# An attention and gated-MLP decode kernel: projection columns dealt p*8+j so that the output leaves without a transpose, and one row of the last weight matrix loaded early in 16 small DMAs

## The chip, the cores and the metric

The kernel runs on one core of a Trainium2 chip. The metric is the device time of one execution in microseconds (us), lower is better. Most executions of one kernel agree within 0.3%. Experiments sent together ran on one chip and share their runs of the kernel before; differences are taken within such a group only.

## The reference

One token is decoded. Block A is attention with 32 query heads on 4 K/V heads over a cache of 65,536 positions. Block B is a small gated MLP. A gate mixes them.

```python
g = sigmoid((x * gate_w).sum(-1))                  # x: [1, 1, 1024]
q = (x @ wq)                                       # wq: [1024, 4096], 32 heads of 128
p = softmax(q @ k_cache.T / sqrt(128))             # caches: [4 heads, 65536, 128] bf16, 64 MB each
a = (p @ v_cache).reshape(4096) @ wo               # wo: [4096, 1024]
b = mlp(x, w_in, w_sp, b_sp) @ w_out               # w_out: [1792, 1024]
out = g * a + (1 - g) * b                          # [1, 1, 1024] bf16
```

About 162 MB are read for 2 KB of output, so the kernel is in the main a stream of loads.

## The kernel before

Every large load goes through one helper on the SP queue, in tiles of 4 MB: 128 partitions with 32 KB each, one packet of 32 KB a partition. Five buffers rotate.

```python
def load(src, shape, name):
    t = kv.tile([P, CT * P], BF16, name=name, tag="kv")        # 5 buffers of 32 KB a partition
    ...
    nc.sync.dma_start(out=v, in_=src)
```

The loads are w_in, wq, then K and V by turns, then w_out, then wo. At the end the output projection runs. It uses blocks of the weight matrix as the stationary operand (each a weight load of 128 x 128 followed by one matmul with 64 copies of a column of the vector), so that the 1024 outputs come to lie in PSUM as 8 columns of 128 partitions:

```python
def project(w, n, vec, c0, first=False, last=False):
    for c in range(n):
        for j in range(NJ):                                     # NJ = 8
            nc.tensor.matmul(
                out_ps[:, j, :], lhsT=w[:, c, j * P:(j + 1) * P],   # 128 neighbouring columns
                rhs=vec[:, c0 + c:c0 + c + 1].to_broadcast([P, W]), ...)

project(load(B_w_out..., "wout_t"), FC, uT, 0, first=True)      # 14 rows per partition
wo_view = A_wo.rearrange("(p c) n -> p c n", c=OC)              # 32 rows of 2 KB per partition
c0 = 0
for split in WO_SPLIT:                                          # ((16,), (8, 4, 2, 1, 1))
    t = kv.tile(...)
    for n in split:
        nc.sync.dma_start(out=t[:, c0 - b:c0 - b + n, :], in_=wo_view[:, c0:c0 + n, :])
        project(t[:, c0 - b:c0 - b + n, :], n, oa, c0, last=(c0 + n == OC))
        c0 += n
out_sb = const.tile([P, NJ], FP32, name="out_sb")
nc.vector.tensor_copy(out=out_sb[:], in_=out_ps[:, :, 0])
outT_ps = psm.tile([NJ, P], FP32, name="outT_ps", tag="m")
nc.tensor.transpose(outT_ps[:], out_sb[:], ident_f[:])
outT = const.tile([NJ, P], BF16, name="outT")
nc.vector.tensor_copy(out=outT[:], in_=outT_ps[:])
nc.sync.dma_start(out=out.rearrange("o t (j p) -> (o t j) p", p=P), in_=outT[:])
```

Column j of `out_ps` holds outputs j*128 to j*128+127, one a partition. The transpose turns that into 8 rows of 256 bytes each.

One more part matters, because it is the only place of this kernel where weight columns are not neighbours: the first MLP matrix, whose stationary blocks take every 14th column (28 bytes apart).

```python
w = win_t[i][:, c, :].rearrange("p (h m f) -> p h f m", h=2, f=FC)       # FC = 14
nc.tensor.matmul(z_ps[...], lhsT=w[:, hf, f, :], rhs=..., ...)
```

Of the kernel before, what the change touches and what calls it, by code (L numbers as in the profile page):

```python
# [7 lines left out]
FP32 = mybir.dt.float32  # L8
BF16 = mybir.dt.bfloat16
# [5 lines left out]
P = 128  # L15
CT = 128
NKV = 5
TG = 8
CPS = 64
LAG = 4  # L20
EVAC_PAT = "vav"
WO_SPLIT = ((16,), (8, 4, 2, 1, 1))
SW = 256
W = 64
WL = 96
# [3 lines left out]
def kernel(  # L29
# [15 lines left out]
    nc = tc.nc  # L45

    _, _, D = A_x.shape
    _, G, S, DH = A_k_cache.shape
# [7 lines left out]
    OC = HD // P  # L56
    NJ = D // P
# [2 lines left out]
    NT = NCG // CT  # L60
    SCALE = float(DH) ** -0.5
    assert DH == P and D % P == 0 and FH % P == 0 and P % H == 0
    assert S % (P * CT) == 0 and CT % CPS == 0 and CPS % TG == 0 and sum(map(sum, WO_SPLIT)) == OC

    const = ctx.enter_context(tc.tile_pool(name="const", bufs=1))
    wk = ctx.enter_context(tc.tile_pool(name="wk", bufs=2))
# [5 lines left out]
    psm = ctx.enter_context(tc.tile_pool(name="psm", bufs=1, space=bass.MemoryType.PSUM))  # L72
# [3 lines left out]
    def load(src, shape, name):  # L76
        t = kv.tile([P, CT * P], BF16, name=name, tag="kv")
        n = 1
        for s in shape:
            n *= s  # L80
        v = t[:, :n]
        if len(shape) == 2:
            v = v.rearrange("p (a b) -> p a b", b=shape[1])
        nc.sync.dma_start(out=v, in_=src)  # L84
        return v

    def load_kv(src, g, j, name):
        k0 = j * CT * P
        return load(src[0, g, k0:k0 + CT * P, :].rearrange("(p c) d -> p c d", c=CT),
                    (CT, DH), name)  # L90

# [37 lines left out]
    def one_hot(shape, dtype, in0, col, name):  # L129
        t = const.tile(shape, dtype, name=name)  # L130
        nc.vector.tensor_scalar(out=t[:], in0=in0, scalar1=pf[:shape[0], col:col + 1],
                                scalar2=None, op0=ALU.is_equal)
        return t
# [4 lines left out]
    ident_f = one_hot([P, P], FP32, row[:], 0, "ident_f")  # L138
# [10 lines left out]
    for t in range(2):  # L149
        nc.vector.tensor_tensor(  # L150
            out=xm[:, t], in0=xb_ps[:, t * P:(t + 1) * P].rearrange("p (i c) -> p c i", c=KC),
# [82 lines left out]
    for c in range(KC):  # L234
        w = wq_t[c // KH]
# [142 lines left out]
    for g in range(G):  # L378
        for j in range(NT):
            ku = k_units(g, j, load_kv(A_k_cache, g, j, "kn"))  # L380
            for _ in ku:
                next(vu, None)
                run_step()
            rest(vu)
            if g > 0:
                vu = v_units(g - 1, j, load_kv(A_v_cache, g - 1, j, "vt"))
# [6 lines left out]
    for j in range(NT):  # L393
        rest(v_units(G - 1, j, load_kv(A_v_cache, G - 1, j, "vt")))


    out_ps = pss.tile([P, NJ, W], FP32, name="out_ps", tag="spt")

    def project(w, n, vec, c0, first=False, last=False):
        for c in range(n):  # L400
            for j in range(NJ):
                nc.tensor.matmul(  # L402
                    out_ps[:, j, :], lhsT=w[:, c, j * P:(j + 1) * P],
                    rhs=vec[:, c0 + c:c0 + c + 1].to_broadcast([P, W]),
                    start=(first and c == 0 and j == 0), stop=(last and c == n - 1),
                    skip_group_check=True)
# [9 lines left out]
    oa = const.tile([P, OC], BF16, name="oa")  # L416
    nc.vector.tensor_scalar(out=oa[:], in0=om_ps[:, :OC], scalar1=rl[:, 0:1], scalar2=gate,
                            op0=ALU.mult, op1=ALU.mult)

    project(load(B_w_out.rearrange("(p c) n -> p c n", c=FC), (FC, D), "wout_t"),  # L420
            FC, uT, 0, first=True)
    wo_view = A_wo.rearrange("(p c) n -> p c n", c=OC)
    c0 = 0
    for split in WO_SPLIT:
        t = kv.tile([P, CT * P], BF16, name="wo_t", tag="kv")
        t = t[:].rearrange("p (c n) -> p c n", n=D)
        b = c0
        for n in split:
            nc.sync.dma_start(out=t[:, c0 - b:c0 - b + n, :], in_=wo_view[:, c0:c0 + n, :])
            project(t[:, c0 - b:c0 - b + n, :], n, oa, c0, last=(c0 + n == OC))  # L430
            c0 += n
    out_sb = const.tile([P, NJ], FP32, name="out_sb")
    nc.vector.tensor_copy(out=out_sb[:], in_=out_ps[:, :, 0])  # L433
    outT_ps = psm.tile([NJ, P], FP32, name="outT_ps", tag="m")
    nc.tensor.transpose(outT_ps[:], out_sb[:], ident_f[:])
    outT = const.tile([NJ, P], BF16, name="outT")
    nc.vector.tensor_copy(out=outT[:], in_=outT_ps[:])
    nc.sync.dma_start(out=out.rearrange("o t (j p) -> (o t j) p", p=P), in_=outT[:])


    last = {}
# [37 lines left out]
```

## Time and profile before

| | before |
|---|---|
| time, median of the runs | 392.84 us |
| profiled span | 390.8 us |
| first 16 rows of wo complete | 377.70 us |
| last arrivals of wo, by DMA engine | 8 at 377.1 to 379.8, 8 at 385.9 to 387.4 us |
| copy of the result out of PSUM starts | 387.93 us |
| output DMA issued, its last arrival | 388.77, 389.96 us |

From the page of the kernel before: the span, the mean busy tenths of the 16 DMA engines in 40 slices, the GB/s in the same slices, and the groups of wo's matmuls and weight loads (busy us, mean ns of one, then idle time before them and its releaser).

```profile
span 390.8 us, 14957 instructions
...
DMA  8999999999999999999999999999999999999972
GB/s 329 426 444 429 441 426 430 434 429 428 429 428 426 431 423 431 429 434 429 424 426 436 424 429 431 423 434 423 428 427 434 436 434 429 434 421 428 433 330 114
...
L402 PE MATMUL out_ps<-oa,wo_t 128*128 128x64 bf16 x256 | 9.7, 204 | 6.1 <-DMA wo_t<-in_A_wo_dram 5.7
L402 PEld LDWEIGHTS <-wo_t 128*128 128x128 bf16 x256 | 9.4, 105 | 6.4 <-DMA wo_t<-in_A_wo_dram 5.8
```

The DMA engines are full from the second slice to the 38th: the load stream sets the time. Only the last two slices are not full. From the groups by line of the same kernel, the weight loads with strided columns (win_t) and with neighbouring ones (wq_t):

```profile
...
L185 PEld LDWEIGHTS <-win_t 128*128 128x128 bf16 x224 | 13.7, 158 | 1.3 <-DMA win_t<-in_B_w_in_dram 0.9 <-issue 0.4
...
L237 PEld LDWEIGHTS <-wq_t 128*128 128x128 bf16 x256 | 7.0, 104 | 7.6 <-DMA wq_t<-in_A_wq_dram 7.6
```

The strided ones have a mean of 158 ns, the others 104 ns. 224 strided pairs keep the engine busy 13.7 us, 61 ns each; 256 contiguous ones 7.0 us, 27 ns each.

The end of the kernel before in the timeline (start us, duration, engine, line, operation):

```profile
...
368.42 3.64 PE L402 MATMUL out_ps<-uT,wout_t 128*128 128x64 bf16 x112
...
377.75 7.13 PE L402 MATMUL out_ps<-oa,wo_t 128*128 128x64 bf16 x182 [5.69 <-DMA wo_t<-in_A_wo_dram]
385.29 2.61 PE L402 MATMUL out_ps<-oa,wo_t 128*128 128x64 bf16 x74 [0.41 <-issue]
...
387.93 0.17 DVE L433 COPY out_sb<-out_ps 128x8 f32<-128x8 f32 x1 [18.79 <-PE out_ps L402]
...
388.15 0.27 PE L435 MATMUL outT_ps<-ident_f,out_sb 128*8 128x128 f32 x1 [0.26 <-DVE out_sb L433]
388.46 0.28 DVE L437 CAST outT<-outT_ps 8x128 bf16<-8x128 f32 x1 [0.37 <-PE outT_ps L435]
388.77 0.36 SPq L438 DMA_DIRECT2D out_dram<-outT  x1
```

PE starts on wo at 377.75, 0.05 us after the first 16 rows are complete, and is done at 387.91, about half a microsecond after the last load (387.43). Copy, transpose, second copy and output DMA follow.

The last stretches of the kernel before. Columns: stretch, its length, busy time and count of PE, weight load, DVE, ACT and POOL, granted TensorE clock, DMA share, GB/s.

```profile
...
370.00:375.00 5.00, 2.06 (x67) 1.94 (x63) 0.00 (x0) 0.00 (x0) 0.00 (x0) 0.90 1.00 424
375.00:380.00 5.00, 2.25 (x43) 2.25 (x44) 0.00 (x0) 0.00 (x0) 0.00 (x0) 0.50 0.70 290
380.00:385.00 5.00, 4.88 (x144) 4.79 (x142) 0.00 (x0) 0.00 (x0) 0.00 (x0) 0.91 0.50 204
385.00:391.00 6.00, 2.88 (x75) 2.46 (x74) 0.45 (x2) 0.00 (x0) 0.00 (x0) 1.00 0.15 57
```

DMA share falls to 0.70 and then 0.50 long before the loads end: half of the engines have finished. The arrival records of wo's last row (one a DMA engine) say the same, eight by 379.8 us and eight more from 385.9 us on. The late ones are, as far as the packets can be told apart, those on which the 55 instruction-fetch packets of 16 KB (about 0.95 us each) fell.

### The profile page before, as it was taken

To read this page: it belongs to the slowest core of one execution; us is meant where nothing else is said; L and a number is where in the kernel's file an instruction comes from. 1 tells how busy PE (TensorE), PEld (TensorE's weight loads), DVE (VectorE), ACT (ScalarE), POOL (GpSimd) and SP (SyncE) were. 2 spreads that over 40 slices of the span, in tenths; PEclk is the share of its full clock that TensorE was granted. 3 is DMA by queue.
4 is the path that set the end of the run, shared out by engine and by line. 5 is a ranking of instruction groups with operands and counts; after the bars stand their busy time and mean duration, and the time that the engine had idled before them with its cause. 6 is when DMAs were issued, how large, how long until landed. Compare 5 with 4: busy or idle time off the path is not lost.

```text
span 390.8 us, 14957 instructions
## 1 busy us (share of the span) xinstructions
PE 306.5 (78%) x7080; PEld 296.8 (76%) x7080; DVE 152.3 (39%) x296; ACT 122.3 (31%) x139; POOL 1.0 (0%) x9
## 2 busy tenths in 40 slices
PE   0774379998888879778888888697979697996946
PEld 0764379887888779778888878696979697896846
DVE  2011036665684335336534543275434345300100
ACT  1010025554574323324543333244524242300000
POOL 1000000000000000000000000000000000000000
PEclk9999999999999989999999999899989899899869
DMA  8999999999999999999999999999999999999972
GB/s 329 426 444 429 441 426 430 434 429 428 429 428 426 431 423 431 429 434 429 424 426 436 424 429 431 423 434 423 428 427 434 436 434 429 434 421 428 433 330 114
DMA packets 6305, 162.96 MB, mean 417 GB/s; under 512 B 740, under 2 KB 740, under 8 KB 1124
## 3 DMA queue, kind: packets, MB, share of 16 engines
q1 hardware_dynamic: 6208, 162.01, 96.8%
q8 instruction: 55, 0.90, 0.8%
q14 instruction: 6, 0.05, 0.0%
q10 hardware_dynamic: 36, 0.00, 0.0%
HBM read 162.01 MB, written 0.00 MB: 415 GB/s over the span
## 4 chain that ended last, share of the span: by engine, by line
PE 55%; DMA 32%; issue 7%; ACT 3%; DVE 1%; SPq 0%; ACTq 0%
PE tps L322 27%; DMA kn<-in_A_k_cache_dram 24%; PE spt L301 13%; PE o_ps L355 11%; DMA wo_t<-in_A_wo_dram 9%; PE out_ps L402 2%; PE o_ps L344 1%; ACT ktt L325 1%; ACT scT L288 1%; ACT scT L307 1%; SPq L84 0%; PE nb_ps L279 0%; DVE mxr L264 0%; DVE mxr L309 0%; PE mxT L271 0%
## 5 line engine op out<-in xcount | busy, mean ns | idle before, releaser
L322 PE MATMUL tps<-ident_b,kn 128*128 128x128 bf16 x2048 | 164.0, 224 | 25.6 <-DMA kn<-in_A_k_cache_dram 12.8
L327 DVE COPY ktt<-tps 128x1024 bf16<-128x1024 bf16 x171 | 116.6, 689 | 123.4 <-PE tps L322 122.9
L322 PEld LDWEIGHTS <-kn 128*128 128x128 bf16 x2048 | 124.0, 100 | 28.8 <-issue 15.3
L325 ACT COPY ktt<-tps 128x1024 bf16<-128x1024 bf16 x85 | 85.9, 1012 | 156.0 <-PE tps L322 156.0
L355 PE MATMUL o_ps<-scT,vt 128*128 128x64 bf16 (+1 forms) x2048 | 104.4, 200 | 14.4 <-issue 11.5
L301 PE MATMUL spt<-qT,ktt 128*128 128x64 bf16 (+7 forms) x2048 | 102.9, 193 | 8.9 <-issue 7.0
L355 PEld LDWEIGHTS <-vt 128*128 128x128 bf16 x2048 | 88.5, 101 | 17.0 <-issue 12.9
L301 PEld LDWEIGHTS <-ktt 128*128 128x128 bf16 x2048 | 85.6, 99 | 10.6 <-issue 8.2
L307 ACT CAST scT<-spt 128x512 bf16<-128x512 f32 x32 | 18.9, 589 | 24.8 <-PE spt L301 15.9
L344 PE MATMUL o_ps<-scT,ones_b 128*128 128x256 bf16 x64 | 18.1, 283 | 2.1 <-issue 1.4
L288 ACT ACTIVATE scT<-scT 128x1024 bf16<-128x1024 bf16 x16 | 16.4, 1056 | 6.2 <-DVE scT L284 6.2
L309 DVE TENSOR_TENSOR mxr<-scT,mxr 128x512 bf16<-128x512 bf16 x24 | 10.2, 425 | 15.8 <-ACT scT L307 14.3
L185 PE MATMUL z_ps<-xT,win_t 128*128 128x18 bf16 x224 | 13.7, 210 | 1.3 <-DMA win_t<-in_B_w_in_dram 0.8
L185 PEld LDWEIGHTS <-win_t 128*128 128x128 bf16 x224 | 13.7, 158 | 1.3 <-DMA win_t<-in_B_w_in_dram 0.9
L402 PE MATMUL out_ps<-oa,wo_t 128*128 128x64 bf16 x256 | 9.7, 204 | 6.1 <-DMA wo_t<-in_A_wo_dram 5.7
L402 PEld LDWEIGHTS <-wo_t 128*128 128x128 bf16 x256 | 9.4, 105 | 6.4 <-DMA wo_t<-in_A_wo_dram 5.8
L237 PE MATMUL q_ps<-xT,wq_t 128*128 128x1 bf16 x256 | 7.1, 165 | 7.5 <-DMA wq_t<-in_A_wq_dram 7.5
L361 DVE TENSOR_TENSOR lm<-sel_q,o_ps 128x32 f32<-128x32 f32 x4 | 0.7, 182 | 31.3 <-PE o_ps L355 31.3
L237 PEld LDWEIGHTS <-wq_t 128*128 128x128 bf16 x256 | 7.0, 104 | 7.6 <-DMA wq_t<-in_A_wq_dram 7.6
L284 DVE TENSOR_TENSOR scT<-scT,negm 128x1024 bf16<-128x1024 bf16 x16 | 10.7, 685 | 0.1
L344 PEld LDWEIGHTS <-ones_b 128*128 128x128 bf16 x64 | 6.4, 100 | 2.3 <-issue 1.6
L433 DVE COPY out_sb<-out_ps 128x8 f32<-128x8 f32 x1 | 0.2, 166 | 18.8 <-PE out_ps L402 18.8
(86 smaller groups left out, 41.6 us busy)
## 6 DMA issues: line engine op xcount, KB each, us to landing
kn<-in_A_k_cache_dram SPq DMA_DIRECT2D x16, 4096.0 KB, 29.6
vt<-in_A_v_cache_dram SPq DMA_DIRECT2D x16, 4096.0 KB, 29.5
wq_t<-in_A_wq_dram SPq DMA_DIRECT2D x2, 4096.0 KB, 29.8
win_t<-in_B_w_in_dram SPq DMA_DIRECT2D x2, 3584.0 KB, 15.2
wo_t<-in_A_wo_dram SPq DMA_DIRECT2D x1, 4096.0 KB, 34.0
wout_t<-in_B_w_out_dram SPq DMA_DIRECT2D x1, 3584.0 KB
wo_t<-in_A_wo_dram SPq DMA_DIRECT2D x1, 2048.0 KB
wo_t<-in_A_wo_dram SPq DMA_DIRECT2D x1, 1024.0 KB
```

What stands on the lines that cost most here:

```text
L185: nc.tensor.matmul(z_ps[:, hf * FC + f, :], lhsT=w[:, hf, f, :], rhs=xT[:, i * KH + c:i * KH + c + 1].to_broadcast([P, zw]), start=(i == 0 ...
L237: nc.tensor.matmul(q_ps[:, h:h + 1], lhsT=w[:, c % KH, h * DH:(h + 1) * DH], rhs=xT[:, c:c + 1], start=(c == 0 and h == 0), stop=(c == KC ...
L284: nc.vector.tensor_tensor(out=blk, in0=blk, in1=negm[:].unsqueeze(1).to_broadcast([P, CT, REP]), op=ALU.add)
L288: nc.scalar.activation(out=blk, in_=blk, func=ACT.Exp, scale=SCALE)
L301: nc.tensor.matmul(spt[g][:, o:o + n], lhsT=ktt[:, j * P:(j + 1) * P], rhs=qT[:, g * REP:g * REP + n], start=True, stop=True, skip_group_c ...
L307: nc.scalar.copy(out=blk, in_=spt[g][:].rearrange("p (c h) -> p c h", h=REP))
L322: nc.tensor.transpose(tps[:, i * P:(i + 1) * P], kn[:, u * TG + i, :], ident_b[:])
L325: nc.scalar.copy(out=ktt[:], in_=tps[:])
L327: nc.vector.tensor_copy(out=ktt[:], in_=tps[:])
L344: nc.tensor.matmul(o_ps[g][:, 2 * WL:], lhsT=ones_b[:], rhs=scT[g][:, j * CT + c:j * CT + c + SW // REP, :].rearrange("p c h -> p (c h)"), ...
L355: nc.tensor.matmul(o_ps[g][:, o0:o0 + wv], lhsT=vt[:, c, :], rhs=scT[g][:, lo:hi, :].rearrange("p c h -> p (c h)"), start=False, stop=(cg ...
L402: nc.tensor.matmul(out_ps[:, j, :], lhsT=w[:, c, j * P:(j + 1) * P], rhs=vec[:, c0 + c:c0 + c + 1].to_broadcast([P, W]), start=(first and ...
```

## The change

Three things are tied together. The output columns are dealt differently: output p*8+j goes to partition p, column j, so that each partition holds 8 neighbouring outputs and can write its 16 bytes straight to the output, with no transpose and no second copy. For that the stationary blocks have to take every eighth column of the weights, 16 bytes apart. And one of wo's 32 rows per partition is brought in early, in 16 small DMAs (of 1 to 15 partitions in turn, and a last one of 8), each ahead of one of the K or V loads; the list at the end of wo has one load fewer.

```diff
-WO_SPLIT = ((16,), (8, 4, 2, 1, 1))
+WO_SPLIT = ((16,), (8, 4, 2, 1))
+LONE = (1, 2, 3, 4, 5, 6, 7, 8, 9, 10, 11, 12, 13, 14, 15, 8)
+LONE_AT = 10
@@
+    lone = const.tile([P, 1, D], BF16, name="lone")
+    lones = [(sum(LONE[:i]), n) for i, n in enumerate(LONE)]
     def load_kv(src, g, j, name):
+        tiles[0] += 1
+        if tiles[0] > LONE_AT and lones:
+            p0, n = lones.pop(0)
+            nc.sync.dma_start(out=lone[p0:p0 + n], in_=wo_view[p0:p0 + n, OC - 1:, :])
@@ def project
+        w = w.rearrange("p c (m j) -> p c j m", j=NJ)
-                    out_ps[:, j, :], lhsT=w[:, c, j * P:(j + 1) * P],
+                    out_ps[:, j, :], lhsT=w[:, c, j, :],
@@
+    project(lone[:], 1, oa, OC - 1)
@@
-    out_sb = const.tile([P, NJ], FP32, name="out_sb")
+    out_sb = const.tile([P, NJ], BF16, name="out_sb")
     nc.vector.tensor_copy(out=out_sb[:], in_=out_ps[:, :, 0])
-    (transpose, second copy, output DMA from 8 rows)
+    nc.sync.dma_start(out=out.rearrange("o t (p j) -> (o t p) j", j=NJ), in_=out_sb[:])
```

More of the change, by code (lines that the diff above doesn't have):

```diff
@@ L62 @@
     assert DH == P and D % P == 0 and FH % P == 0 and P % H == 0
-    assert S % (P * CT) == 0 and CT % CPS == 0 and CPS % TG == 0 and sum(map(sum, WO_SPLIT)) == OC
+    assert S % (P * CT) == 0 and CT % CPS == 0 and CPS % TG == 0 and sum(map(sum, WO_SPLIT)) + 1 == OC and sum(LONE) == P
     const = ctx.enter_context(tc.tile_pool(name="const", bufs=1))
@@ L85, in load @@
         return v
+    wo_view = A_wo.rearrange("(p c) n -> p c n", c=OC)
+    lone = const.tile([P, 1, D], BF16, name="lone")
+    lones = [(sum(LONE[:i]), n) for i, n in enumerate(LONE)]
+    tiles = [0]
     def load_kv(src, g, j, name):
         k0 = j * CT * P
+        tiles[0] += 1
+        if tiles[0] > LONE_AT and lones:
+            p0, n = lones.pop(0)
+            nc.sync.dma_start(out=lone[p0:p0 + n], in_=wo_view[p0:p0 + n, OC - 1:, :])
         return load(src[0, g, k0:k0 + CT * P, :].rearrange("(p c) d -> p c d", c=CT),
@@ L421 @@
             FC, uT, 0, first=True)
-    wo_view = A_wo.rearrange("(p c) n -> p c n", c=OC)
+    project(lone[:], 1, oa, OC - 1)
     c0 = 0
@@ L429 @@
             nc.sync.dma_start(out=t[:, c0 - b:c0 - b + n, :], in_=wo_view[:, c0:c0 + n, :])
-            project(t[:, c0 - b:c0 - b + n, :], n, oa, c0, last=(c0 + n == OC))
+            project(t[:, c0 - b:c0 - b + n, :], n, oa, c0, last=(c0 + n == OC - 1))
             c0 += n
-    out_sb = const.tile([P, NJ], FP32, name="out_sb")
+    out_sb = const.tile([P, NJ], BF16, name="out_sb")
     nc.vector.tensor_copy(out=out_sb[:], in_=out_ps[:, :, 0])
-    outT_ps = psm.tile([NJ, P], FP32, name="outT_ps", tag="m")
-    nc.tensor.transpose(outT_ps[:], out_sb[:], ident_f[:])
-    outT = const.tile([NJ, P], BF16, name="outT")
-    nc.vector.tensor_copy(out=outT[:], in_=outT_ps[:])
-    nc.sync.dma_start(out=out.rearrange("o t (j p) -> (o t j) p", p=P), in_=outT[:])
+    nc.sync.dma_start(out=out.rearrange("o t (p j) -> (o t p) j", j=NJ), in_=out_sb[:])
     last = {}
```

## The prediction

> **What bounds the kernel now.** The load stream: in the table of slices the 16 DMA engines are busy 9/10 or more in every slice from the second to the 38th, at about 430 GB/s, while PE, DVE and ACT are not full. The end differs. By stretches, DMA share is 1.00 until 375 us, 0.70 in 375-380 and 0.50 in 380-385. The records of the single engines' arrivals say why: of the sixteen arrivals of wo's last row, eight come at 377.1-379.8 us, eight at 385.9-387.4. Instruction-fetch packets (16 KB, 55 of them, about 0.95 us each) fall on the same eight engines in turn[...].
>
> Then, from the timeline: wo's first 16 rows land at 377.7; PE multiplies from 377.75, first at clock 0.5 (about 44 ns a pair), later 26.5 ns; the last copy starts at 387.93, 0.5 us after the last arrival. Transpose and second copy follow; the output DMA issues at 388.77; its last arrival is at 389.96. So at the end PE is only just behind the loads, with almost no slack.
>
> **Removed.** Transpose and second copy: 388.77 - 387.93 = 0.84 us becomes about 0.3: -0.55 us.
>
> **Moved.** 256 KB of wo go early. [...] last landing -0.1 to -0.4 us; wo's first 16 rows land up to 0.5 us later. The bulk stream loses nothing to the small issues: SP mostly waits for buffers.
>
> **Added.** Every weight load of the projection now takes columns 16 bytes apart. The only strided weight load in this trace is win_t's (28 bytes apart): 112 pairs took 6.8 us at clock 1.0, 61 ns a pair, against 27 ns for contiguous wq_t (128 in 3.49 us). [...] wout's 112 pairs: 3.6 to 7 us, hidden before 377.7. But wo's remaining 31 rows, 248 pairs from about 378.0: 248 x 61 ns = 15.1 us, end near 393.1, perhaps 0.5-1 later if the start runs at clock 0.5, against 387.75 now. The projection, not the loads, ends last. Output DMA: 128 pieces of 16 B instead of 8 of 256 B: +0 to 0.3 us.
>
> **Sum.** +5.5 (PE) -0.55 +0.15: about +5. With a chance of one in five that 16 bytes costs little (then about -0.5 us, 392.2) and about one in seven that it costs more than 28 (then 400-408): predicted 397.6 us, range 392.0 to 401.0; faster by over 2%: 0.01, within 2%: 0.83, slower: 0.16.
>
> **What would show it.** wo_t pairs at about 61 ns, weight-load mean near 158 instead of 98-105 ns; PE busy without gap from 378 to 393, the loads all landed by 387.3; the chain of waits ending in the projection, no DMA wait near the end; copy to output issue 0.3 us; first group of engines later by up to 0.6 us, second earlier by up to 0.6.
>
> **What would make it wrong.** Weight load at 16 bytes as quick as contiguous (then the end stays load-bound and gains half a microsecond)[...]; 16-byte output pieces costing over a microsecond[...].

The sum came to about +5 us: +5.5 for PE, -0.55 for the transpose and second copy, +0.15 for the output DMA. None of these terms is cut. Cut are the reason why columns 16 bytes apart should cost as much as those 28 bytes apart, and the numbers of the late engines with the sharing of the moved rows among the engines, from which came the landing figures (last landing 0.1 to 0.4 us earlier, first 16 rows up to 0.5 us later, groups of engines 0.6 us either way). What is left of both is the author's estimate: the 61 ns a pair are those of win_t at 28 bytes, and nothing measured stood behind the landing figures or the 0 to 0.3 us for the output pieces. That SP mostly waits for buffers is in the trace: 257.3 us of its issues' waits in the kernel before are for the transposes of K (L322).

## The result

The changed kernel takes 399.25 us (median of 4; 399.10 to 399.55) against 392.84 (median of 4; 392.73 to 392.94): 6.4 us more, ratio 1.0164, 95% interval 1.0146 to 1.0182: slower beyond the noise, by less than 2%. A ratio here and below is the mean time of one kernel's fast runs over that of the other's of the same rounds, so it is not quite the ratio of the medians.

From the page of the changed kernel, the lines that answer to those of before:

```profile
span 397.6 us, 14968 instructions
...
DMA  8999999999999999999999999999999999999960
GB/s 332 450 429 420 424 439 433 437 419 430 433 430 425 407 417 428 423 436 441 427 422 420 422 431 431 414 420 422 424 436 427 420 427 402 422 438 429 424 281 7
...
L414 PE MATMUL out_ps<-oa,wo_t 128*128 128x64 bf16 x248 | 15.1, 230 | 3.0 <-DMA wo_t<-in_A_wo_dram 3.0
L414 PEld LDWEIGHTS <-wo_t 128*128 128x128 bf16 x248 | 15.0, 170 | 3.1 <-DMA wo_t<-in_A_wo_dram 3.1
```

And from its groups by line, win_t and wq_t, which the change does not touch:

```profile
...
L196 PEld LDWEIGHTS <-win_t 128*128 128x128 bf16 x224 | 13.7, 158 | 1.0 <-DMA win_t<-in_B_w_in_dram 0.6 <-issue 0.4
...
L248 PEld LDWEIGHTS <-wq_t 128*128 128x128 bf16 x256 | 7.0, 104 | 7.8 <-DMA wq_t<-in_A_wq_dram 7.8
```

wo's weight loads went from a mean of 105 ns to 170 ns, and their busy time from 9.4 to 15.0 us for 8 fewer. win_t and wq_t are as before. The end in the timeline:

```profile
...
369.53 6.93 PE L414 MATMUL out_ps<-uT,wout_t 128*128 128x64 bf16 x112 [0.98 <-DMA wout_t<-in_B_w_out_dram]
...
379.93 15.09 PE L414 MATMUL out_ps<-oa,wo_t 128*128 128x64 bf16 x248 [2.99 <-DMA wo_t<-in_A_wo_dram]
395.05 0.17 DVE L445 CAST out_sb<-out_ps 128x8 bf16<-128x8 f32 x1 [25.95 <-PE out_ps L414]
395.25 0.35 SPq L446 DMA_DIRECT2D out_dram<-out_sb  x1
```

PE multiplies without a gap from 379.93 to 395.02 us: 248 pairs in 15.09 us, 60.8 ns each. The last load of wo is complete at 388.98 us, six microseconds before the copy; the end is set by the projection and no longer by the loads. In the stretches:

```profile
...
375.00:380.00 5.00, 2.01 (x34) 1.91 (x33) 0.00 (x0) 0.00 (x0) 0.00 (x0) 1.00 0.96 409
380.00:385.00 5.00, 5.00 (x84) 5.00 (x85) 0.00 (x0) 0.00 (x0) 0.00 (x0) 0.66 0.68 282
385.00:390.00 5.00, 5.00 (x87) 5.00 (x87) 0.00 (x0) 0.00 (x0) 0.00 (x0) 1.00 0.27 106
390.00:395.00 5.00, 5.00 (x84) 4.91 (x82) 0.00 (x0) 0.00 (x0) 0.00 (x0) 1.00 0.01 3
```

And one stretch of it in which the granted clock was 0.5:

```profile
...
381.00:383.50 2.50, 2.50 (x45) 2.50 (x44) 0.00 (x0) 0.00 (x0) 0.00 (x0) 0.50 0.66 274
```

The stretch at clock 0.5 has 45 recorded pairs in 2.5 us; four stretches of the same length from 384 to 394 us, at clock 1.0, have 45, 45, 46 and 45. The pace of strided pairs did not depend on the granted clock here. That of contiguous pairs did: in the kernel before, 42 were recorded in the 2 us from 378.5 to 380.5 at clock 0.5, and 102 in the 3 us from 381.5 to 384.5 at clock 1.0. (Some records are missing in both.)

All of the 6.8 us between the two profiled spans can be laid out along the end:

| term | before | changed | difference | predicted |
|---|---|---|---|---|
| first 16 rows of wo complete | 377.70 | 379.88 | +2.18 | +0.3, at most +0.5 |
| from there to the copy | 10.23 | 15.17 | +4.94 | about +4.9 (end near 393.1, less the +0.3 above) |
| copy to output issue | 0.84 | 0.20 | -0.64 | -0.55 |
| output issue to last arrival | 1.19 | 1.42 | +0.23 | 0 to +0.3 |
| last arrival to the end of the span | 0.83 | 0.88 | +0.05 | not named |

Of the four terms that the prediction named, three are as predicted. The first is not: loads that have nothing to do with the projection came 2.2 us later.

### The profile page after: what moved, and what is told of

Its sections match the earlier page's. It is cut to its first block, busy times and chain, and to the rows that moved or that the text cites. A ratio compares the mean times of both kernels' runs of the same rounds, so it can differ in the third digit from the quotient of the medians.

```text
span 397.6 us, 14968 instructions
## 1 busy us (share of the span) xinstructions
PE 310.0 (78%) x7079; PEld 300.4 (76%) x7079; DVE 152.1 (38%) x295; ACT 122.4 (31%) x139; POOL 1.0 (0%) x9
## 4 chain that ended last, share of the span: by engine, by line
PE 64%; DMA 20%; issue 12%; ACT 2%; DVE 1%; SPq 0%; ACTq 0%
PE tps L333 30%; PE spt L312 15%; PE o_ps L366 13%; DMA kn<-in_A_k_cache_dram 12%; DMA wo_t<-in_A_wo_dram 8%; PE out_ps L414 4%; PE o_ps L355 1%; ACT ktt L336 1%; ACT scT L299 1%; SPq L86 0%; ACT scT L318 0%; PE nb_ps L290 0%; DVE mxr L275 0%; DVE mxr L320 0%; PE mxT L282 0%
## 5 line engine op out<-in xcount | busy, mean ns | idle before, releaser
L333 PEld LDWEIGHTS <-kn 128*128 128x128 bf16 x2048 | 122.7, 100 | 25.3 <-issue 18.9
L366 PE MATMUL o_ps<-scT,vt 128*128 128x64 bf16 (+1 forms) x2048 | 101.3, 197 | 16.4 <-issue 14.3
L366 PEld LDWEIGHTS <-vt 128*128 128x128 bf16 x2048 | 85.2, 98 | 19.1 <-issue 16.3
L312 PEld LDWEIGHTS <-ktt 128*128 128x128 bf16 x2048 | 84.7, 99 | 18.2 <-issue 15.9
L414 PE MATMUL out_ps<-oa,wo_t 128*128 128x64 bf16 x248 | 15.1, 230 | 3.0 <-DMA wo_t<-in_A_wo_dram 3.0
L414 PEld LDWEIGHTS <-wo_t 128*128 128x128 bf16 x248 | 15.0, 170 | 3.1 <-DMA wo_t<-in_A_wo_dram 3.1
L372 DVE TENSOR_TENSOR lm<-sel_q,o_ps 128x32 f32<-128x32 f32 x4 | 0.7, 182 | 26.9 <-PE o_ps L366 26.9
L414 PE MATMUL out_ps<-uT,wout_t 128*128 128x64 bf16 x112 | 6.9, 236 | 1.0 <-DMA wout_t<-in_B_w_out_dram 1.0
## 6 DMA issues: line engine op xcount, KB each, us to landing
win_t<-in_B_w_in_dram SPq DMA_DIRECT2D x2, 3584.0 KB, 15.1
```

What stands on the lines that cost most here:

```text
L312: nc.tensor.matmul(spt[g][:, o:o + n], lhsT=ktt[:, j * P:(j + 1) * P], rhs=qT[:, g * REP:g * REP + n], start=True, stop=True, skip_group_c ...
L333: nc.tensor.transpose(tps[:, i * P:(i + 1) * P], kn[:, u * TG + i, :], ident_b[:])
L366: nc.tensor.matmul(o_ps[g][:, o0:o0 + wv], lhsT=vt[:, c, :], rhs=scT[g][:, lo:hi, :].rearrange("p c h -> p (c h)"), start=False, stop=(cg ...
L414: nc.tensor.matmul(out_ps[:, j, :], lhsT=w[:, c, j, :], rhs=vec[:, c0 + c:c0 + c + 1].to_broadcast([P, W]), start=(first and c == 0 and j ...
```

## The experiments

Twelve kernels ran, in four groups. The packet counts below are taken from the records of single DMA packets in each profile. A 32 KB packet takes 1.213 us (the median in every kernel). Packets that met an instruction fetch take about 1.7 us, 57 of them before (55 of the 57 overlap a fetch in time); the interesting ones are those between 1.24 and 1.64 us, of which the kernel before has 5 and the changed kernel 228.

| kernel | time, us | before in the same group | ratio, 95% interval | packets of 1.24 to 1.64 us: count, excess over 1.213 us |
|---|---|---|---|---|
| the change | 399.25 | 392.84 | 1.0164 [1.0146, 1.0182] | 228, 19.4 us |
| stride_only | 397.68 | 392.85 | 1.0120 [1.0104, 1.0135] | 26, 2.9 us |
| lone_only | 394.40 | 392.85 | 1.0040 [1.0027, 1.0053] | 211, 20.0 us |
| direct_only | 392.44 | 392.85 | 0.9984 [0.9972, 0.9997] | 6, 1.5 us |
| lone_one_dma | 393.02 | 392.85 | 1.0006 [0.9993, 1.0018] | 9, 2.5 us |
| lone_flip | 395.81 | 392.99 | 1.0071 [1.0058, 1.0084] | 356, 30.0 us |
| lone_flip_dest | 395.14 (one run) | 392.99 | - | 361, 26.9 us |
| stride4 | 394.12 | 392.99 | 1.0028 [1.0016, 1.0040] | 8, 1.5 us |
| rebalance | 420.42 | 392.99 | 1.0691 [1.0665, 1.0718] | 7, 1.3 us (and 186 longer ones, see there) |
| lone16 | 395.42 | 392.96 | 1.0057 [1.0024, 1.0091] | 309, 25.7 us |
| lone16_step8 | 394.38 | 392.96 | 1.0028 [0.9998, 1.0058] | 120, 6.0 us |
| shifted | 404.81 | 392.96 | 1.0295 [1.0267, 1.0324] | 121, 14.2 us |
| low2 | 396.09 | 392.96 | 1.0083 [1.0069, 1.0097] | 65, 9.8 us |

The excess is a sum over 16 engines: 19.4 us is 1.2 us an engine.

### Each part by itself: lone_only, stride_only, direct_only, lone_one_dma

lone_only is the changed kernel with contiguous weights and the transposed output of before:

```diff
-        w = w.rearrange("p c (m j) -> p c j m", j=NJ)
-                    out_ps[:, j, :], lhsT=w[:, c, j, :],
+                    out_ps[:, j, :], lhsT=w[:, c, j * P:(j + 1) * P],
     (and the transpose, second copy and output DMA of before)
```

> The kernel before with the early last row (16 small DMAs) alone; weights contiguous, output transposed. Theory S (the strided weight loads cost nearly all of the +6.4 us; the small DMAs are harmless): time within 0.4 us of before, last arrival of wo 0.1 to 0.4 us earlier, wo pairs 26.5 ns. Rival D (the small DMAs disturb the load stream, and the later landing of wo's first 16 rows, 379.9 against 377.7 us, is theirs): 1.0 to 2.5 us slower than before, with many 32 KB packets over 1.24 us, as in the changed kernel (301 against 62).

Measured: 1.55 us slower, 211 slow packets with 20 us of excess. From its timeline:

```profile
...
379.79 9.78 PE L413 MATMUL out_ps<-oa,wo_t 128*128 128x64 bf16 x248 [4.32 <-DMA wo_t<-in_A_wo_dram]
389.61 0.17 DVE L444 COPY out_sb<-out_ps 128x8 f32<-128x8 f32 x1 [17.31 <-PE out_ps L413]
```

The first 16 rows arrive at 379.74 us, 2.0 us later than before, and the last of wo's loads at 388.89 us instead of 387.43: theory D holds, S does not. The small DMAs are the cause of the late landing, without any help from the projection.

stride_only is the kernel before with the strided weights and the direct output:

```diff
+        w = w.rearrange("p c (m j) -> p c j m", j=NJ)
-                    out_ps[:, j, :], lhsT=w[:, c, j * P:(j + 1) * P],
+                    out_ps[:, j, :], lhsT=w[:, c, j, :],
     (and the direct output of the change)
```

> Strided weights and direct output without the early row. Theory S: the projection needs 256 x 61 ns = 15.6 us from the landing of wo's first 16 rows, so +5.0 to +5.3 us against before (397.8 to 398.1), the load stream as in before (first rows at 377.7). Rival D: the same +5 us here, the remaining 1.3 us of the changed kernel being the small DMAs'. A second rival, that the later landing comes from the strided projection itself, would give the full +6.4 us here.

```profile
...
377.73 15.57 PE L403 MATMUL out_ps<-oa,wo_t 128*128 128x64 bf16 x256 [2.62 <-DMA wo_t<-in_A_wo_dram]
393.34 0.17 DVE L434 CAST out_sb<-out_ps 128x8 bf16<-128x8 f32 x1 [24.40 <-PE out_ps L403]
393.53 0.35 SPq L435 DMA_DIRECT2D out_dram<-out_sb  x1
```

Measured: 4.8 us slower. PE starts at 377.73 as before and needs 15.57 us for 256 pairs, 60.8 ns each. The load stream is undisturbed. This part and lone_only add up to the whole: 4.83 + 1.55 = 6.38 us, and the change measured 6.41. That the sum is so close is partly luck, because the row costs time by different ways. In lone_only the end follows the last landing of wo, which is 1.46 us later than before. In the changed kernel it follows the landing of the first 16 rows, 2.18 us later than before, less the 8 pairs of 61 ns that the early row takes out of the end (0.49 us).

direct_only keeps the contiguous weights and takes the direct output alone. Its values come out permuted.

```diff
-    (transpose, second copy, output DMA of before)
+    nc.sync.dma_start(out=out.rearrange("o t (p j) -> (o t p) j", j=NJ), in_=out_sb[:])
```

> Contiguous weights, output written straight from the copied columns: wrong on purpose (the values come in permuted order), to time the direct output by itself. Both theories: copy to output issue falls from 0.84 to 0.20 us, issue to landing rises from 1.19 to about 1.42 us; net -0.3 to -0.5 us against before.

```profile
...
377.78 10.44 PE L402 MATMUL out_ps<-oa,wo_t 128*128 128x64 bf16 x256 [5.71 <-DMA wo_t<-in_A_wo_dram]
388.26 0.17 DVE L433 CAST out_sb<-out_ps 128x8 bf16<-128x8 f32 x1 [19.11 <-PE out_ps L402]
388.45 0.35 SPq L434 DMA_DIRECT2D out_dram<-out_sb  x1
```

Measured: 0.4 us faster (interval 0.03% to 0.28%). The copy is followed by the issue after 0.19 us, and the last arrival comes 1.41 us after the issue (389.86 in the arrival records). So this is all that the transpose was worth. Taken from stride_only, it leaves 5.2 us for the strided weight loads.

lone_one_dma is lone_only with `LONE = (128,)`: the same row, early, in one DMA.

> As lone_only, but the early row comes in one DMA of 128 partitions instead of 16 small ones. Theory S: equal to before within 0.3 us. Rival D: equal to before here, while lone_only is 1 us or more slower. If both are slower by the same, it is the moving of the row or the changed numbering of later DMAs, not the small sizes.

Measured: 0.2 us slower, interval includes 1; 9 slow packets. Moving the row costs next to nothing, sending it in 16 small DMAs costs 1.5 us.

### What about the small DMAs: lone_flip and lone_flip_dest

In lone_only the slow packets came in bursts. The packets of the small DMAs can be seen themselves (2 KB, 0.084 us), so each burst can be laid beside its DMA. That of 10 partitions, at 223 us, has the first, of 9 packets; those of 12 to 15 partitions, from 242.5 us on, and the last of 8, at 283 us (22 packets), have nearly all the rest. Those of 1 to 9 partitions, which write partitions 0 to 44, and that of 11 had at most 3 each. (The expectation below says 11 to 15.)

```diff
-    lones = [(sum(LONE[:i]), n) for i, n in enumerate(LONE)]
+    lones = [(P - sum(LONE[:i + 1]), n) for i, n in enumerate(LONE)]          # lone_flip
-            nc.sync.dma_start(out=lone[p0:p0 + n], in_=...)
+            nc.sync.dma_start(out=lone[P - p0 - n:P - p0], in_=...)           # lone_flip_dest
```

> lone_only took 1.55 us more than before; there, bursts of 32 KB packets of 1.25 to 1.36 us instead of 1.213 stood at 222 to 285 us, where the small DMAs of 11 to 15 partitions and the last of 8 ran; that of 8 partitions in the middle made none. Here the sizes come in the same order of time, but from the top partition down (1 writes partition 127, ... 15 partitions 8 to 22, the last 8 partitions 0 to 7). Theory size: the DMAs of 12 to 15 partitions slow the stream: bursts again at 240 to 285 us, time about +1.5 us. Theory place: DMAs whose partitions are 64 or higher slow it: no bursts after 240 us, bursts between 140 and 215 us instead.

> As lone_only in sizes and source rows, but each small DMA writes the mirrored partitions (wrong on purpose: the rows land in the wrong partitions). If the place matters by its destination in SBUF, bursts move to before 215 us, as theory place says of lone_flip. If it matters by its source in HBM, bursts stay at 240 to 285 us here and move in lone_flip. Theory size: bursts at 240 to 285 us in both.

Measured: neither theory. In lone_flip the bursts start at 166.5 us (4 packets) and 185 us (20 packets), with the DMAs of 4 to 6 partitions, and go on to 281 us; 356 slow packets, 2.8 us slower. In lone_flip_dest, they start at 174 us and go on to 281 us; 361 slow packets. So small DMAs of 6 to 9 partitions make bursts of 16 to 27 packets when they write partitions 83 to 112, and have at most 3 when they write 15 to 44. The last DMA, of 8, has 22 at partitions 120 to 127 in lone_only and 3 at 0 to 7 in each of the two others. This speaks for place and against size; but those of 12 to 15 make bursts also below 64, which the place theory as stated rules out. (The record counts lone_flip_dest as correct although its row lands in the wrong partitions.) What the pair does settle is the side: the two have the same destinations and different source rows, and look alike, while lone_flip_dest and lone_only have the same source rows and differ. The destination in SBUF decides, the source in HBM does not, as far as one profile of each can tell.

### Neighbouring partitions: rebalance, lone16 and lone16_step8

Half of the DMA engines finish 6 to 10 us early, so there was a version to try that was meant to give them more: rebalance sends the first 48 partitions of wo's 16 rows in six DMAs of 8 partitions. That such DMAs run on the early engines was the author's estimate; no run shows it, and the conditions that rested on engine numbers are cut below, with the second outcome (396 us).

```diff
+EIGHTS = {16: 6}
@@
-            nc.sync.dma_start(out=t[:, c0 - b:c0 - b + n, :], in_=wo_view[:, c0:c0 + n, :])
+            e = EIGHTS.get(n, 0)
+            for p in range(0, 8 * e, 8):
+                nc.sync.dma_start(out=t[p:p + 8, ...], in_=wo_view[p:p + 8, c0:c0 + n, :])
+            nc.sync.dma_start(out=t[8 * e:, ...], in_=wo_view[8 * e:, c0:c0 + n, :])
```

> The kernel before, with the first 48 partitions of wo's 16-row load sent as six DMAs of 8 partitions, the other 80 as one: [...] the early group of arrivals moves 3 packets of 32 KB (3.6 us) later and the late group 3.6 us earlier: last arrival of wo near 383.8 instead of 387.4 us, time 3.0 to 3.8 us below before (389.0 to 389.8).[...]

Measured: 27 us slower. 186 packets of 32 KB took over 1.64 us. 55 of them came before 356 us and have met an instruction fetch, as in the kernel before; the other 131, after 356 us, have a mean of 2.67 us, and the longest took 3.86. From 357 us on the packets of w_out (28 KB) are slow as well, up to 3.15 us instead of 1.06: the small DMAs slow the large loads beside them and not only themselves. From its page, and from its timeline:

```profile
...
DMA  8999999999999999999999999999999999999970
GB/s 352 417 433 441 422 437 426 423 442 428 427 423 437 430 415 433 426 433 431 426 439 415 436 435 417 442 415 437 437 414 445 415 433 432 246 200 183 206 211 31
```

```profile
...
404.49 6.91 PE L403 MATMUL out_ps<-oa,wo_t 128*128 128x64 bf16 x181 [20.39 <-DMA wo_t<-in_A_wo_dram]
...
414.61 0.42 PE L403 MATMUL out_ps<-oa,wo_t 128*128 128x64 bf16 x8 [0.20 <-DMA wo_t<-in_A_wo_dram]
```

The first rows came at 404.4 instead of 377.7 us. The rate fell from 427 GB/s (350 to 356 us) to 283 (356 to 361 us), when of wo only the six small DMAs, to partitions 0 to 47, had been issued; the seventh, with the other 80 partitions, followed at 360.96 us. What is shown is that DMAs of eight neighbouring partitions were slow: 1.213 us for 32 KB in the large loads, mostly 2.0 to 3.5 us here. (Issues had to wait for an old DMA here too, 17.1 us for w_out, but the DMA share was 0.85 to 1.09 in all stretches of 5 us from 356 to 401 us: the engines were not idle.) By what mechanism is not shown, and neighbouring partitions alone do not explain all: in lone_only 8 rows to the neighbouring partitions 28 to 35 made no burst, and 8 to 120 to 127 did.

lone16 and lone16_step8 test on the change's own row, with equal sizes and numbers of DMAs, whether neighbouring partitions do the harm:

```diff
-LONE = (1, 2, 3, ..., 15, 8)
+LONE = (16,) * 8                                                                    # both
-            nc.sync.dma_start(out=lone[p0:p0 + n], in_=wo_view[p0:p0 + n, OC - 1:, :])
+            r = p0 // n                                                             # lone16_step8
+            nc.sync.dma_start(out=lone[r::8], in_=wo_view[r::8, OC - 1:, :])
```

In each of the two expectations the first outcome goes with harm from neighbouring destinations; "uneven" puts the harm down to the sizes in lone_only (unequal, and under 16 partitions).

> As lone_only, but the early row comes in 8 DMAs of 16 neighbouring partitions[...]: bursts of packets over 1.24 us at each of the 8 DMAs, and 0.6 us or more slower than before. Theory uneven[...]: no bursts, within 0.3 us of before.

> As lone16, but each of the 8 DMAs takes every eighth partition (r, r+8, ... r+120), so that its rows go to partitions far apart. [...] clearly fewer slow packets than lone16 and a time at least 0.3 us nearer to before. Theory count (every extra DMA costs the stream something, wherever it writes): the same as lone16.

Measured: lone16 2.5 us slower by the medians, with 309 slow packets of mean 1.27 to 1.32 us in its bursts: the eight DMAs are all of 16 partitions here, so neither unequal nor smaller sizes are needed for the harm. lone16_step8 1.4 us slower by the medians (its interval just includes no difference, and its overlap with lone16's leaves the times alone unclear), with 120 slow packets and 6.0 us of excess instead of 25.7; most of its bursts have means of 1.24 to 1.28 us. By the packets, spreading the partitions takes away three quarters of the harm. The step spreads the source rows in HBM too; that the source does not matter rests on lone_flip_dest. As to the time, what remains above before is not explained by the packets.

### Weight columns 8 bytes apart: stride4

```diff
+DEAL = 4
+        w = w.rearrange("p c (a m b) -> p c a b m", m=P, b=DEAL)
-                    out_ps[:, j, :], lhsT=w[:, c, j * P:(j + 1) * P],
+                    out_ps[:, j, :], lhsT=w[:, c, j // DEAL, j % DEAL, :],
+    nc.sync.dma_start(out=out[0, 0, :].rearrange("(a p b) -> p a b", p=P, b=DEAL),
+                      in_=out_sb[:].rearrange("p (a b) -> p a b", b=DEAL))
```

> The kernel before with weight columns 4 elements (8 bytes) apart and the output written straight, in pieces of 8 bytes, two a partition; no early row. [...] pairs of 27 to 40 ns, the projection stays behind the loads only slightly, and the time is 0.1 to 0.5 us below before. If any step above one element costs the same 61 ns, +4.8 us as in stride_only.

From the groups by line of stride4, and its timeline:

```profile
...
L404 PEld LDWEIGHTS <-wo_t 128*128 128x128 bf16 x256 | 9.8, 120 | 5.8 <-DMA wo_t<-in_A_wo_dram 5.5 <-issue 0.2
```

```profile
...
368.61 3.90 PE L404 MATMUL out_ps<-uT,wout_t 128*128 128x64 bf16 x112
...
377.93 10.18 PE L404 MATMUL out_ps<-oa,wo_t 128*128 128x64 bf16 x256 [5.43 <-DMA wo_t<-in_A_wo_dram]
...
388.14 0.17 DVE L435 CAST out_sb<-out_ps 128x8 bf16<-128x8 f32 x1 [18.82 <-PE out_ps L404]
388.33 0.41 SPq L436 DMA_DIRECT2D out_dram<-out_sb  x1
```

Measured: the weight loads are almost free, mean 120 ns against 105 with neighbouring columns and 170 at 16 bytes (w_out's: 118 against 98 and 171); wout's 112 pairs take 3.90 us, 35 ns each, against 3.64 us before. So the cost is not that of any stride: a step of 8 bytes takes 35 ns a pair, one of 16 bytes 60.8 (stride_only), one of 28 bytes 61 (win_t). (No step between 4 and 8 elements was run.) The kernel was still 1.1 us slower than before, and the timeline shows why: the copy starts at 388.14, the output DMA is issued at 388.33, and its last arrival is at 391.32 us, 3.0 us later (1.19 before, 1.42 with pieces of 16 bytes). Writing 256 pieces of 8 bytes costs more (1.8 us) than is saved from copy to issue (0.84 to 0.19 us). The expected gain was wrong for that reason.

### A version meant to beat both: shifted and low2

Both move some of wo's rows that belong to partitions 64 to 127 onto partitions 0 to 63, and load them by DMAs of 8 partitions four apart, to keep clear of the neighbouring partitions of rebalance. The forecasts count on the moved rows going from the late engines to the early ones: the author's estimate, not shown by any run.

```diff
+LOW = 8                                        # shifted; low2: 2, and early, one ahead of each K/V load
+    nc.tensor.matmul(om_ps[:HP, OC + 1:2 * OC + 1], lhsT=lm[...][:, HP:], rhs=sel_c[:], ...)   # upper half
+            for r in [32 * a + i for a in range(2) for i in range(4)]:
+                nc.sync.dma_start(out=t[r:r + 29:4].rearrange("p (h c) n -> p h c n", h=2),
+                    in_=wo_view.rearrange("(h p) c n -> p h c n", h=2)[r:r + 29:4, :, c0:c0 + LOW, :])
+            project(t[:HP, :LOW, :], LOW, oa, c0)
+            project(t[:HP, LOW:2 * LOW, :], LOW, oa2, c0)
```

> A version meant to beat both kernels: the kernel before, where for 8 of wo's 32 rows per partition the half that belongs to partitions 64 to 127 is put on partitions 0 to 63 instead (with a copy of the vector's upper half brought there by two more matmuls), loaded by DMAs of 8 partitions four apart (0, 4, ... 28)[...]. If [...] the trouble of rebalance was its neighbouring partitions, the late group ends 4.8 us earlier and the early group 4.8 us later: last arrival 382.6 to 384.6, time 2.5 to 3.8 us below before (389.0 to 390.3). If neighbouring partitions were not the trouble of rebalance, packets are as slow as there and the time is 10 us or more above before.

Measured: 11.9 us slower. The packets are the part that went right: all of the 16 KB packets of these DMAs have a median of 0.611 us, the same as in the kernel before. Spacing the partitions by four did remove what rebalance suffered from. The loss is elsewhere. The issues on SP in the timeline, and its waits:

```profile
...
350.57 0.33 SPq L451 DMA_DIRECT2D wo_t<-in_A_wo_dram  x1
356.94 23.82 SPq L442 DMA_DIRECT2D wo_t<-in_A_wo_dram  x8
380.87 2.53 SPq L451 DMA_DIRECT2D wo_t<-in_A_wo_dram  x4
```

```profile
...
SPq L442 <- DMA wo_t<-in_A_wo_dram: 9.2, 1, 9.2
...
SPq L442 <- DMA wout_t<-in_B_w_out_dram: 7.8, 1, 7.8
```

The eight small DMAs take from 356.94 to 380.76 us to be issued. Two of the issues waited for older loads, each the eighth DMA before it on SP: the seventh 7.8 us for w_out and the eighth 9.2 us for wo's first 16 rows. The four loads behind them were issued from 380.87 us on, and the engines ran partly empty: the DMA share was 0.78 to 0.80 from 375 to 385 us and 0.48 from 387 to 392.

low2 was to avoid that:

> The idea of shifted without its blocked issue: 2 of wo's 32 rows per partition (their upper halves moved to partitions 0 to 63), in 8 DMAs of 8 partitions four apart, one ahead of each of the last loads of K and V as in the changed kernel. In shifted such packets took 611 ns for 16 KB, as quick as in the large loads, where rebalance's took 2.1 to 3.3 us for 32 KB; so no bursts here. [...] Expected: last arrival of wo 386.1 to 386.4 instead of 387.4 us, time 0.8 to 1.3 us below before (391.7 to 392.2). If the small DMAs disturb wherever they write: 1 us or more above before, as lone_only.

Measured: 3.1 us slower. The expectation was wrong, and the cause is open. Its small DMAs were issued from 235 us on, but more than half of the excess of its 32 KB packets over the kernel before (24 of 43 us) lies before 235 us, where both kernels issue the same loads: the instruction fetches are longer in this build (median 1.06 us against 0.96), and the packets that meet them have a mean of 1.88 us against 1.72, and 84 of them instead of 57. shifted shows the same (1.02 us, 1.92 us, 90). Neither run tells what makes fetches longer, so low2 does not say whether evenly spread small DMAs are harmless.

No correct version beat the kernel before. direct_only is 0.4 us faster, but its values are permuted.

## Why the prediction was right or wrong

- **The bound, and the strided weight loads: right.** Predicted 248 x 61 ns = 15.1 us; measured 15.09. The win_t lines of the same kernel (28 bytes apart) gave the size; that 16 bytes would cost as much was an estimate, which stride_only and the changed kernel bear out (60.8 ns a pair in both). stride4 bounds it from the other side: 35 ns a pair at 8 bytes. Why the step matters so is not shown. Half speed of the clock at the start, which the prediction allowed 0.5 to 1 us for, did not matter to strided pairs (45 in 2.5 us at clock 0.5 as at 1.0). The mean of one weight load was 170 ns and not near 158 as forecast; the pace of the pairs, which sets the time, was as forecast.
- **The end becomes the projection's: right.** PE has no gap from 379.93 to 395.02, and the loads are complete six microseconds earlier than the copy.
- **The direct output: right.** -0.64 us to the issue, +0.23 us for 128 pieces of 16 bytes; by itself -0.4 us.
- **The early row: the step that failed.** The prediction put it as "The bulk stream loses nothing to the small issues: SP mostly waits for buffers", and expected wo's first 16 rows "up to 0.5 us later" and the last landing 0.1 to 0.4 us earlier. The 16 small DMAs cost 1.55 us by themselves; the first rows came 2.0 us later in lone_only (2.2 in the changed kernel), the last 1.5 us later. It was the issue that was looked at, and no cost of it shows; the cost is in the packets of the large loads, which take longer beside the small DMAs, and it depends on where in SBUF these write. lone_flip_dest, lone16 against lone16_step8, and rebalance against shifted (mostly 2.0 to 3.5 us for 32 KB at neighbouring partitions, 0.611 us for 16 KB at spread ones) show that. The mechanism is not shown, and why small DMAs of up to 9 partitions did no harm at partitions 0 to 44 is open. In the changed kernel the early group of engines also came 3.8 to 4.8 us later (1.1 to 2.0 in lone_only), where up to 0.6 was forecast; what made the rest is not known.
- **The late engines: right as far as shown.** The prediction placed the instruction fetches on eight engines and put the late arrivals down to them; in lone_only, as far as its packets can be linked, 50 of 55 fetches lie on the eight late chains. The numbers that it gave these engines no run here gives. Nor do small DMAs keep to one group in lone_only: the DMA of 8 partitions at the end sent 5 packets with the early engines, 1 in the middle and 2 with the late ones; that of 15 partitions sent 6, 1 and 8.
- **The sum.** Predicted +4.8 us (397.6), measured +6.4 (399.25), inside the range of 392.0 to 401.0. The difference is 1.65 us; the first term of the table above was missed by 1.9, and lone_only puts a price of 1.55 us on the early row, so the row is the greater part of it. The central value had also been drawn down by a chance of one in five that the stride costs nothing.

## What to carry to other kernels

Before a layout is changed to save a transpose, look at which operand pays for it: here 0.4 us at the end was bought with a stride of one element per 16 bytes in 360 weight loads, and where PE has no slack those 34 ns each are the time. Small DMAs that look free at the issue are to be judged by what they do to the large loads beside them: here, some that wrote a few neighbouring partitions slowed these (rebalance, lone16) and others did not (up to 9 rows at partitions 0 to 44), and the packets' durations showed it where the times alone were unclear. And when a change has several parts, run each by itself: here the two parts account for the whole, and one of them was thought to be a gain.
